# Causal masks of the third and fourth chunk pair as products on TensorE, with the first part of the hand-written order rearranged

## The chip, the cores and the metric

The kernel runs on one core of one Trainium2 chip. The metric is the device time of one execution in microseconds (us); lower is better. A core has five engines that work beside each other and wait for one another by semaphores: TensorE (PE, matrix products; the loads of its stationary operand are shown as PEld), VectorE (DVE), ScalarE (ACT), GpSimd (POOL) and SyncE (SP), whose queue here issues nearly all DMAs.

## The reference

Two layers in a row: a gated state-space scan in chunks (batch 4, 8 heads, 768 tokens, head size 32, state size 16), and a feed-forward block (3072 tokens, model size 256, hidden size 1536). The three weight matrices come as float64.

```python
for c in range(nc):                                   # chunks of 32 tokens
    cum = np.cumsum(la, axis=-1)                      # la = log(clip(a))
    L = np.exp(cum[:, :, :, None] - cum[:, :, None, :])
    L = L * causal                                    # causal: i >= j
    M = np.einsum('bhin,bhjn->bhij', Cc, Bc) * L
    y_intra = np.einsum('bhij,bhjd->bhid', M, xc)
    y_inter = np.einsum('bhin,bhnd->bhid', Cc, state) * decay_to_i[:, :, :, None]
    y[:, :, sl] = y_intra + y_inter
    state = decay_full[:, :, None, None] * state + np.sum(Bx, axis=2)
...
x = y.transpose(0, 2, 1, 3).reshape(3072, 256)
xn = x / np.sqrt(np.mean(x * x, axis=-1, keepdims=True) + 1e-06) * rms_g
g = xn @ w_gate
out = (g * (1.0 / (1.0 + np.exp(-g))) * (xn @ w_val)) @ w_out
```

## The kernel before, in words

**Work.** The scan is computed in chunks of 128 tokens, and for later pairs in halves of 64; two chunks are a *pair*, and there are twelve pairs. Two pairs make a token block of 512 tokens, and the feed-forward block runs on the six of them in turn. The steps of block 0, which also hold the scan of pairs 2 and 3, are the start of everything: constants are built, the weights are fetched in 18 pieces and made from float64 into float32 by hand, and the scan's first pairs run meanwhile.

**Order.** Nothing is scheduled by a planner. One long string, `order`, names the steps, as `block:kind.numbers/slot`, and a loop at the end of the kernel calls each in turn. Each step issues its instructions on its engines' queues, so that string is the order of work on every engine and on SP's DMA queue; an engine that waits holds up all that is queued behind it. Tiles come from pools with a fixed number of buffers, and a new tile waits until the buffer that it is given is free. The number behind the slash is one of three slots, each a pair of PSUM banks, that a step takes and a later one gives back.

**Steps that matter here.**
- `fetch.k` issues the DMA of weight piece k into one of six buffers (`wr`). Pieces 0 and 1 hold 128 columns of both the gate and the value matrix; pieces 2 to 11 hold 256 columns of one of them in turn (2 gate, 3 value, 4 gate and so on); 12 to 17 are the output matrix. `man.k` (DVE, lines 216 and 219) takes the mantissa, `pow.k` (ACT, three passes, line 197) the power of two, and `wt.k` (DVE, line 225) multiplies the two into the float32 weight.
- `bc.p` and `x.p` fetch B, C and x of pair p; `scale.p` (DVE, line 514) scales B; `turn.p` transposes B and C on PE, and `T`, `Tt`, `Td` bring them to SBUF. `rowout`, `rowe`, `dT` and `spread` send rows of decays to DRAM and back in another shape.
- `r.k` and `parts.k` make sums of logs and split them in two bfloat16 parts on DVE (lines 384 to 391). `sums` (lines 461 and 468) adds them up in PSUM for each head by small products, and `exp` (line 476) takes the exponential into the tile `L`.
- **The mask.** For pairs 0 and 1 `mask` first writes, for each chunk, the product of an identity with `whole16`, which is 0 where i >= j and -2^100 elsewhere, so that the exponential is 0 there (line 447). For pairs 2 and 3 there is no such product: `sums` opens the banks itself, and after the exponential `causal` (line 482) selects on GpSimd, once for each half of 64 partitions, over 16 x 64 elements a partition. Pairs from 4 on get their decays another way and use the same `causal`.
- `g` and `gg` are the products of B and C, and `L` and `L1` multiply them by the decays on DVE (lines 612 to 624). `A` and `S` carry the state, `y` is the output of a pair, `sq`, `yt`, `ms`, `rs`, `xn` the norm (`rs` takes the roots on ACT, line 809; `xn.0` is line 831 on DVE).
- `early.f.s` are the first gate and value products of columns f on half s of the tokens, made before the norm is known (line 855); `norm.f` corrects them (line 866). `gate.f` (line 845) does columns 2 to 5 after the norm. From column 6 on, block 0, like all later blocks, uses a product scheme with seven products for eight: `P.k.j` (line 931), `take` (line 937), `C` (line 943), `silug` and `hidg`, with weight sums by `cw` on DVE or `cwp` on GpSimd (line 900) and token sums by `tx` or `txp` (line 908). `o.f` is the output product (line 963).

Of the kernel before, what the change touches and what calls it, by code (L numbers as in the profile page):

```python
# [20 lines left out]
def kernel(  # L21
# [423 lines left out]
    def mask(e):  # L445
        for i in range(2):
            nc.tensor.matmul(out=e[:, i], lhsT=ident16,
                             rhs=whole16.unsqueeze(1).to_broadcast([P, 4, P]),
                             start=True, stop=False, skip_group_check=True)

    def sums(p, half, e):
# [6 lines left out]
        for k, h in enumerate(heads):  # L458
            for i, r in enumerate(rows_of):
                for u in parts:  # L460
                    nc.tensor.matmul(out=e[u, i, k * n:(k + 1) * n],
                                     lhsT=sel[r, h:h + 1].to_broadcast([32, n]),
                                     rhs=row[r, 0, u], start=p >= 2 and k == 0, stop=False,
                                     tile_position=(r.start, u.start), skip_group_check=True)
# [759 lines left out]
    def of_chunk(n, fn):  # L1224
# [31 lines left out]
        0:idle.7 0:x.0 0:hmask 1:exps 0:head 0:fetch.0 0:never 0:whole16 0:mask.0.0/0 0:aT  # L1256
        0:mask.1.1/2 0:gcol 0:part 0:fetch.2 0:after 0:part2 0:tmask 0:sel 0:upto 0:mean 0:mid
        0:mask.0.1/1 0:mids 0:la0 0:log4.4.2 0:log4.0.4 0:r.0 0:log 0:after2 0:x.1 0:upto2 0:parts.0
        0:d 0:dx 0:eps 0:scale.0 0:middles 0:c*2 0:turn.0 0:fetch.1 0:sums.0.1 0:cx 0:Tb.0 0:exp.0.1
        0:sums.0.0 0:exp.0.0 0:turn.1 0:Tt.1.0 0:Tt.1.1 0:T.0 0:T.1 0:last.0 0:g.0.1/1 0:Tl.0  # L1260
        0:scale.1 0:pow.0 0:cc 0:man.0 0:bc.2 0:L.0.1 0:g.0.0/0 0:fetch.5 0:A.0 0:sums.1.1 0:exp.1.1
        0:S.0 0:last.1 0:row.1 0:L.0.0 0:mask.1.0/1 0:sums.1.0 0:man.2 0:rowout.1 0:wt.0 0:exp.1.0
        0:rowe.1 0:g.1.1/0 0:Tl.1 0:g.1.0/2 0:log4.6.2 0:L.1.0 0:A.1 0:y.0/1 0:fetch.3 0:L.1.1 0:S.1
        0:y.1/2 0:pow.2 0:sq.0 0:yt.0 0:sq.1 0:man.1 0:row.0 0:rowe.0 0:r.1 0:parts.1 0:early.0.0/0
        0:bc.3 0:yt.1 0:ms.0 0:wt.2 0:scale.2 0:sums.3/1 0:pow.1 0:sums.2/2 0:pow.5 0:exp.3
        0:rowout.0 0:rs.0 0:tok 0:fetch.8 0:tokout 0:man.3 0:pow.3 0:early.0.1 0:wt.1 0:early.1.0/1
        0:dT.3 0:xn.0 0:turn.2 0:norm.0 0:T.2 0:turn.3 0:T.3 0:Tt.3.1 0:fetch.4 0:dT.2 0:man.5
        0:early.1.1 0:fetch.9 0:exp.2 0:Tt.2.0 0:fetch.7 0:wt.3 0:wt.5 0:Tt.2.1 0:norm.1 0:tx.0.0
        0:Tt.3.0 0:Td.3 0:Td.2 0:man.4 0:fetch.6 0:gate.2/0 0:silu.0 0:hid.0 0:gg.2/1 0:L1.2.3
        0:L1.2.2 0:L.2.0 0:pow.4 0:wt.4 0:man.7 0:gate.3/2 0:pow.7 0:wt.7 0:ydone.1 0:fetch.11  # L1270
        0:cwp.1.0 0:man.9 0:man.8 0:gate.4/1 0:silu.2 0:hid.2 0:x.2 0:pow.8 0:wt.8 0:txp.0.1 0:pow.9
        0:man.6 0:A.2 0:silu.3 0:x.3 0:wt.9 0:pow.6 0:hid.3 0:gate.5/0 0:S.2 0:cwp.4.0 0:silu.4
        0:scale.3 0:table.1 0:y.2/2 0:hid.4 0:silu.5 0:wt.6 0:cwp.3.0 0:hid.5 0:ydone.0 0:tx.0.2
        0:pow.11 0:S.3 0:cw.3.1 0:man.11 0:sq.2 0:bc.4 0:switch.1 0:P.2.3 0:switch.0 0:P.1.3 1:dT.0
        0:take.1.3 0:C.11.3 0:P.1.4 0:take.1.4 0:P.2.4 0:C.11.4 0:yt.2 0:x.4 0:silu.1 0:P.6.3
        0:take.6.3 0:cwp.3.2 0:tx.0.3 0:cw.4.1 0:fetch.10 0:gg.3/2 1:table 0:wt.11 0:P.5.3 0:P.7.3
        0:cwp.3.3 0:man.10 0:pow.10 0:wt.10 0:bc.5 0:cwp.5.0 0:take.7.3 0:C.22.3 0:fetch.14
        0:silug.22.3 0:silug.11.4 0:L1.3.3 0:P.5.4 0:L1.3.2 0:P.6.4 0:take.6.4 0:scale.5 0:L.3.0
        0:P.4.3 0:silug.21.3 0:P.3.3 0:scale.4 0:hidgp.11.4 0:cwp.4.2 0:fetch.12 0:pow.12
        0:hidg.21.3 0:cw.4.3 0:x.5 0:C.12.3 0:silug.12.3 0:y.3/2 0:silug.11.3 0:P.7.4 0:take.7.4  # L1280
        0:cw.5.1 1:dT.1 0:cwp.5.2 1:S.0 0:fetch.15 0:P.1.5 0:P.2.5 0:hidg.12.3 0:cwp.5.3 1:spread.0
        0:P.4.4 0:fetch.13 0:spread.10 0:take.1.5 0:P.6.5 0:table.0 0:spread.11 1:S.1 0:C.11.5
        0:C.22.4 0:sq.3 0:yt.3 0:ms.1 0:rs.1 0:cwp.1.2 0:man.12 0:take.6.5 0:P.5.5 0:wt.12 0:cwp.1.1
        0:hid.1 0:P.3.4 0:man.13 0:hidgp.11.3 1:turn.1 0:silug.21.4 0:P.7.5 0:take.7.5 1:spread.1
        0:o.0/2 0:cw.0.0 0:hidg.22.3 0:man.15 0:o.1 0:P.4.5 0:C.22.5 0:hidg.21.4 0:pow.13 0:wt.13
        0:P.3.5 0:C.12.4 0:silug.22.4 0:hidgp.22.4 0:man.14 0:silug.21.5 0:silug.22.5 0:silug.11.5
        0:C.12.5 0:pow.14 0:hidg.21.5 0:fetch.17 0:pow.15 0:o.2 0:cw.0.1 0:rb.1 0:o.3 0:xn.1 1:P.1.0
        0:silug.12.5 0:wt.14 0:hidgp.11.5 0:man.17 1:bc.0 1:take.1.0 1:P.1.1 0:tx.1.0 1:P.2.1 1:T.1
        0:txp.1.1 0:o.4 0:tx.1.2 1:take.1.1 1:P.6.1 0:pow.17 1:cw.2.0 0:hidgp.22.5 0:tx.1.3 1:C.11.1
        1:silu.11.1 1:P.6.0 1:sub.0 1:P.2.0 0:wt.15 0:wt.17 1:turn.0 1:C.11.0 0:cwp.0.2 1:Tt.1.0  # L1290
        1:hid.11.1 1:take.6.0 1:P.7.0 1:take.7.0 1:take.6.1 1:silu.11.0 1:P.5.1 1:P.5.0 1:P.4.0
        1:C.22.0 0:cwp.0.3 0:fetch.16 1:silu.21.0 0:spread.9 1:P.7.1 1:P.3.0 1:cwp.2.2 1:hid.21.0
        0:ydone.3 0:silug.12.4 1:take.7.1 1:hid.11.0 1:cwp.2.1 0:o.5 1:P.1.3 1:Tt.1.1 1:Td.1
        0:cw.1.3 1:C.22.1 1:P.4.1 1:bc.1 1:P.3.1 0:man.16 0:hidg.12.5 0:o.6 0:o.7 1:T.0 1:Tt.0.0
        0:subp.9 1:twop.2 0:hidg.12.4 0:pow.16 0:subp.11 1:take.1.3 1:C.12.0 1:silu.12.0 1:silu.21.1
        1:hidp.12.0 1:silu.22.0 1:hid.21.1 0:wt.16 1:two.0 1:two.1 1:x.0 1:silu.22.1 1:two.4
        1:C.12.1 1:twop.6 1:hid.22.0 0:ex.9 1:P.2.3 1:P.1.2 1:C.11.3 1:P.6.3 1:ex.0 1:silu.11.3
        1:P.2.2 1:take.1.2 1:P.5.3 1:hid.11.3 1:silu.12.1 1:scale2.1 1:take.6.3 1:P.7.3 1:take.7.3
        1:C.22.3 1:hid.12.1 0:o.8 1:P.6.2 0:sub.10 1:twop.3 1:take.6.2 1:C.11.2 1:two.9 1:P.4.3
        1:silu.21.3 1:two.8 1:cwp.2.3 1:hid.21.3 0:o.9 1:P.1.4 1:silu.11.2 1:hid.11.2 1:spread.3  # L1300
        1:sub.3 1:ex.3 1:P.3.3 1:take.1.4 1:twop.5 1:Tt.0.1 1:Td.0 1:C.12.3 1:silu.12.3 1:hidp.12.3
        0:ex.10 2:dT.0 1:P.5.2 1:P.6.4 1:take.6.4 1:P.7.2 1:take.7.2 0:ex.11 1:P.2.4 0:o.10 0:o.11
        1:C.22.2 1:silu.22.2 1:spread.2 1:P.4.2 1:two.10 1:silu.22.3 0:spread.8 0:subp.8 0:put.0
        1:P.3.2 0:put.1 0:put.2 1:hidp.22.1 0:ydone.2 1:C.11.4 1:silu.11.4 1:P.5.4 1:P.7.4 1:sub.2
        1:silu.21.2 1:hid.21.2 1:hid.11.4 1:hidp.22.3 0:put.3 0:ex.8 0:exps 1:hidp.22.2 1:scale2.0
        2:dT.1 1:P.1.5 1:g 1:C.12.2 1:ex.2 1:L1.3 1:take.1.5 1:P.6.5 1:take.7.4 1:C.22.4 1:twop.7
        1:silu.22.4 1:P.2.5 1:P.4.4 1:take.6.5 1:L 1:L1.2 1:P.7.5 1:y.0 1:C.11.5 1:silu.21.4
        1:hid.21.4 1:x.1 1:silu.11.5 1:P.5.5 1:two.11 1:take.7.5 1:hid.22.4 1:O.2.0 1:hid.11.5
        1:silu.12.2 1:hidp.12.2 1:u.0 1:P.4.5 1:silu.21.5 1:O.2.1 1:O.15.0 1:O.15.1 1:w.0 1:w.2
        1:C.22.5 1:silu.22.5 2:S.0 1:y.1 1:hid.21.5 1:u.1 1:O.3.0 1:u.2 2:bc.1 1:u.3 1:O.3.1 2:S.1  # L1310
        1:O.0.0 1:O.0.1 2:spread.2 2:spread.1 1:subp.1 1:P.3.5 1:C.12.5 1:sq 1:up.4 1:w.4 1:O.17.0
        1:O.17.1 1:yt 1:silu.12.5 1:hid.12.5 1:w.5 1:up.5 1:ms 1:rs 1:hidp.22.5 1:P.3.4 1:C.12.4
# [146 lines left out]
```

## Time and profile before

| what | value |
|---|---|
| time, median of 3 runs | 396.28 us (396.26 to 396.57) |
| the profiled execution's own time | 397.5 us |
| its span, first to last instruction | 395.8 us |
| PE busy, share of the span | 387.3 us, 98% |
| DVE busy | 287.4 us, 73% |
| ACT busy | 233.6 us, 59% |
| POOL busy | 155.5 us, 39% |
| granted TensorE clock | 1.000 |

The span leaves out what lies before the first and behind the last instruction, 1.7 us in the profiled execution. Busy shares are averages over the whole span; the views by stage, further down, part the start (constants, weights, first pairs) from the rest. A row of the timeline reads: start, duration, engine, line, operation, output <- inputs, shapes, count, and in brackets the idle time of the engine before it with what ended it. Rows of one line that follow each other are merged, so "x8" is eight instructions from the first one's start to the last one's end.

### The profile page before, as it was taken

How to read it: one execution, taken by the hardware profiler on the slowest of the kernel's cores; microseconds unless marked ns; L12 is line 12 of the kernel's file. 1: busy time of each engine (PE TensorE's matmuls, PEld its weight loads, DVE VectorE, ACT ScalarE, POOL GpSimd, SP SyncE). 2: the span in 40 equal slices, each digit the busy share in tenths (PEclk: the TensorE clock that was granted, in tenths of full speed). 3: DMA queues.
4: the chain of work that ended last, by engine and by line, in shares of the span. 5: the costliest groups of instructions: out<-in, count | busy, mean ns of one | idle time of the engine just before them, and what ended most of it. 6: DMA issues, size and time to landing. Idle time of an engine off the chain costs nothing.

```text
span 395.8 us, 9624 instructions
## 1 busy us (share of the span) xinstructions
PE 387.3 (98%) x3833; PEld 333.0 (84%) x3833; DVE 287.4 (73%) x594; ACT 233.6 (59%) x483; POOL 155.5 (39%) x172
## 2 busy tenths in 40 slices
...
GB/s 101 189 165 295 181 216 190 132 154 71 23 1 68 57 87 131 84 2 30 107 36 82 13 2 68 2 15 36 42 1 3 0 8 27 55 0 2 2 2 53
DMA packets 92533, 27.01 MB, mean 68 GB/s; under 512 B 77416, under 2 KB 86344, under 8 KB 92488
## 3 DMA queue, kind: packets, MB, share of 16 engines
...
q10 hardware_dynamic: 2080, 0.13, 0.4%
...
## 4 chain that ended last, share of the span: by engine, by line
PE 80%; DVE 7%; ACT 6%; issue 2%; SPq 2%; DMA 2%; POOL 0%; DVEq 0%; ACTq 0%
PE gate L931 28%; PE o L1052 20%; PE val L931 20%; PE o L963 5%; PE y L716 3%; ACT e L197 3%; DMA wr<-in_moe_w_val_dram 2%; PE g L579 1%; SPq L125 1%; DVE wgv L225 1%; DVE m L219 1%; PE tp L529 1%; ACT u L197 1%; DVE L L618 1%; DVE ob L1083 1%
## 5 line engine op out<-in xcount | busy, mean ns | idle before, releaser
L943 DVE TENSOR_TENSOR c<-val,p 128x512 f32<-128x512 f32 x99 | 67.3, 686 | 40.4 <-PE val L931 28.6
L937 ACT COPY p<-gate 128x512 f32<-128x512 f32 x99 | 56.7, 583 | 57.1 <-PE gate L931 55.6
L956 POOL TENSOR_TENSOR hid<-c 128x256 f32<-128x256 f32 x40 | 33.6, 847 | 90.4 <-ACT c L197 88.2
L931 PE MATMUL gate<-tx,wgv 128*128 128x256 f32 x264 | 65.9, 382 | 0.0
L197 ACT ACTIVATE c<-c 128x256 f32<-128x256 f32 x99 | 39.1, 415 | 30.5 <-DVE c L943 30.1
L931 PEld LDWEIGHTS gate<-tx,wgv 128*128 128x128 f32 x264 | 48.9, 190 | 7.2 <-issue 0.3
L956 DVE TENSOR_TENSOR hid<-c 128x256 f32<-128x256 f32 x59 | 28.5, 492 | 16.9 <-ACT c L197 16.9
L1083 DVE TENSOR_TENSOR ob<-ob,o 128x128 f32<-128x128 f32 (+1 forms) x90 | 24.4, 298 | 21.1 <-PE o L1052 17.7
L482 POOL TENSOR_SCALAR_AFFINE_SELECT L<-L 64x512 f32<-64x512 f32 (+1 forms) x36 | 28.2, 783 | 21.7 <-ACT L L197 19.0
L1052 PE MATMUL o<-two,hid 128*128 128x128 f32 x280 | 36.3, 276 | 0.3 <-DVE ob L1083 0.2
L1052 PEld LDWEIGHTS o<-two,hid 128*128 128x128 f32 x280 | 34.4, 192 | 1.5 <-DVE ob L1083 0.4
L931 PE MATMUL val<-tx,sw 128*128 128x256 f32 x132 | 34.0, 382 | 0.0
L931 PE MATMUL val<-xn,sw 128*128 128x256 f32 x132 | 33.7, 380 | 0.0
L931 PE MATMUL val<-xn,wgv 128*128 128x256 f32 x132 | 33.3, 380 | 0.2 <-ACT u L197 0.2
L931 PE MATMUL gate<-tx,sw 128*128 128x256 f32 x132 | 33.4, 381 | 0.0
L931 PE MATMUL gate<-xn,wgv 128*128 128x256 f32 x132 | 32.9, 379 | 0.0
L197 ACT ACTIVATE u<-gate 128x256 f32<-128x256 f32 (+1 forms) x37 | 14.8, 403 | 22.8 <-PE gate L931 20.9
L931 PEld LDWEIGHTS val<-tx,sw 128*128 128x128 f32 x132 | 24.8, 190 | 4.0 <-DVE c L943 0.5
L931 PEld LDWEIGHTS val<-xn,wgv 128*128 128x128 f32 x132 | 24.9, 190 | 3.6 <-ACT u L197 0.3
L931 PEld LDWEIGHTS gate<-tx,sw 128*128 128x128 f32 x132 | 24.6, 190 | 3.4 <-issue 0.2
L931 PEld LDWEIGHTS gate<-xn,wgv 128*128 128x128 f32 x132 | 24.6, 190 | 3.2
L931 PEld LDWEIGHTS val<-xn,sw 128*128 128x128 f32 x132 | 24.5, 190 | 3.2 <-issue 0.2
(196 smaller groups left out, 738.5 us busy)
## 6 DMA issues: line engine op xcount, KB each, us to landing
...
wr<-in_moe_w_out_dram SPq DMA_DIRECT2D x6, 512.0 KB
...
wr<-in_moe_w_gate_dram SPq DMA_DIRECT2D x5, 512.0 KB, 8.0
wr<-in_moe_w_val_dram SPq DMA_DIRECT2D x5, 512.0 KB, 4.6
...
```

The lines of the kernel that those rows point to most:

```text
L125: queue.dma_start(out=st[p][name][:, i], in_=src[b, :, sl, :].rearrange("h s n -> s h n"))
L197: nc.scalar.activation(**operands)
L219: nc.vector.scalar_tensor_tensor(out=f, in0=lo.bitcast(U32), scalar=2.0 ** -32, in1=m, op0=ALU.mult, op1=ALU.add)
L482: nc.gpsimd.affine_select(out=L[r], in_=L[r], pattern=[[0, L.shape[1]], [1, HC]], compare_op=ALU.is_ge, fill=0.0, base=0, channel_multipli ...
L716: nc.tensor.matmul(out=y[2 * k + u][rows, (2 * n + i) * HC:(2 * n + i + 1) * HC], start=(k, u, rows.start) not in opened, stop=True, skip_ ...
L931: nc.tensor.matmul(out=dst[:, half[w]], lhsT=lhsT, rhs=rhs, start=(k in (1, 2, 5) and w == 0), stop=True, skip_group_check=True)
L937: nc.scalar.copy(out=t, in_=Xs[j])
L943: nc.vector.tensor_tensor(out=t, in0=Zs[j], in1=a, op=ALU.add)
L956: engine.tensor_tensor(out=hid[:, 2 * j + c // 10 - 1, c % 10 - 1], in0=u, in1=src[:, half[1]], op=ALU.mult)
L963: nc.tensor.matmul(out=o, lhsT=hid[:, f, k // 2, (k % 2) * P:(k % 2 + 1) * P], rhs=wo[:, f], start=opens, stop=(f == NF - 1), skip_group_c ...
L1052: nc.tensor.matmul(out=Os[blk, b][:, place * P:(place + 1) * P], lhsT=hidden_or_sum(u)[:, g], rhs=rhs, start=(blk, b) not in opened, stop= ...
L1083: nc.vector.tensor_tensor(out=o, in0=o, in1=src, op=ALU.add if what[0] == "+" else ALU.subtract)
```

## The change

The masks of pairs 2 and 3 become products like those of pairs 0 and 1: a new constant `never16` (128 x 64, bfloat16) holds the mask of a 64-token half in each half of the partitions, two copies on DVE make it (`mask16`), and `mask.2` and `mask.3` write two products each (128 x 512, bfloat16) into the slot that `sums` then adds to. The two selections on GpSimd behind each of `exp.2` and `exp.3` are gone (four instructions). `sums` no longer takes a slot nor opens the banks.

The order's steps from the 14th to about the 310th are rearranged: 311 steps become 314 (`never16`, `mask.2` and `mask.3` are new). Among them some change their engine: from DVE to GpSimd go the token sums `tx.0.0` and `tx.0.3`, the weight sums `cw.4.1`, `cw.4.3`, `cw.5.1` and the products `hidg.12.3` and `hidg.22.3`; from GpSimd to DVE go the weight sums `cwp.4.0`, `cwp.3.2`, `cwp.1.1`, `cwp.1.2` and the product `hidgp.11.4`. The steps from `0:o.1 0:P.4.5` on are the same as before.

```diff
+    never16 = const.tile([P, HC], BF16, name="never16")
...
+    def mask16():
+        for r in halves:
+            nc.vector.tensor_copy(out=never16[r], in_=never[r, r])
...
-    def mask(e):
+    def mask(p, e):
+        m = [P, 4, P] if p < 2 else [P, NH, HC]
         for i in range(2):
             nc.tensor.matmul(out=e[:, i], lhsT=ident16,
-                             rhs=whole16.unsqueeze(1).to_broadcast([P, 4, P]),
+                             rhs=(whole16 if p < 2 else never16).unsqueeze(1).to_broadcast(m),
                              start=True, stop=False, skip_group_check=True)
...
-                                     rhs=row[r, 0, u], start=p >= 2 and k == 0, stop=False,
+                                     rhs=row[r, 0, u], start=False, stop=False,
...
         activation(out=L.rearrange("p i h m -> p i (h m)"), in_=e, func=AF.Exp)
-        if p >= 2:
-            causal(L.rearrange("p i h m -> p (i h) m"))
...
-    def start_decays(p, half):
+    def start_decays(p, half=0):
         ps["e", p, half] = e = take("e", ("e", p, half))
-        mask(e)
-
-    def sums_of_decays(p, half=0):
-        if p >= 2:
-            ps["e", p, half] = take("e", ("e", p, half))
-        sums(p, half, ps["e", p, half])
+        mask(p, e)
...
-        "sums": sums_of_decays,
+        "sums": lambda p, half=0: sums(p, half, ps["e", p, half]),
```

The first part of the new order (the steps up to `gate.2`; before it the 13 unchanged ones from `0:warm` to `0:idle.7`):

```
0:gcol 0:x.0 0:never 0:after 0:fetch.0 0:fetch.1 0:x.1 0:whole16 0:mask.0.0/0
0:part 0:hmask 0:upto 0:mid 0:mids 0:part2 0:aT 0:mask.1.1/2 0:la0 0:log4.0.4 0:upto2 0:r.0
0:fetch.2 0:head 0:sel 0:middles 0:after2 0:fetch.3 0:log4.4.2 0:log4.6.2 0:bc.3 0:tmask
0:parts.0 0:log 0:c*2 0:cx 0:mask.0.1/1 0:turn.0 0:Tb.0 0:T.0 0:d 0:dx 0:sums.0.1 0:sums.0.0
0:exp.0.1 0:never16 1:exps 0:exp.0.0 0:turn.1 0:scale.1 0:last.1 0:cc 0:scale.0 0:T.1 0:mean
0:g.0.1/1 0:Tt.1.0 0:g.0.0/0 0:Tt.1.1 0:L.0.1 0:L.0.0 0:sums.1.1 0:exp.1.1 0:row.1
0:rowout.1 0:man.0 0:bc.2 0:mask.1.0/1 0:sums.1.0 0:rowe.1 0:g.1.1/0 0:L.1.1 0:Tl.1
0:g.1.0/2 0:exp.1.0 0:L.1.0 0:fetch.4 0:last.0 0:Tl.0 0:fetch.7 0:dT.2 0:tok 0:tokout 0:A.1
0:A.0 0:S.0 0:S.1 0:pow.0 0:wt.0 0:y.0/1 0:sq.0 0:pow.1 0:y.1/2 0:sq.1 0:row.0 0:yt.0
0:man.1 0:wt.1 0:mask.3/1 0:rowe.0 0:yt.1 0:ydone.1 0:r.1 0:man.3 0:scale.3 0:eps
0:early.0.0/0 0:early.0.1 0:rowout.0 0:ms.0 0:parts.1 0:pow.3 0:pow.2 0:wt.3 0:rs.0
0:mask.2/2 0:scale.2 0:man.2 0:wt.2 0:sums.3 0:sums.2 0:exp.3 0:turn.2 0:T.2 0:Tt.2.0 0:xn.0
0:turn.3 0:norm.0 0:T.3 0:Tt.3.1 0:Tt.2.1 0:fetch.5 0:Tt.3.0 0:exp.2 0:Td.2 0:early.1.0/1
0:early.1.1 0:dT.3 0:man.4 0:table.1 0:x.2 0:norm.1 0:man.5 0:Td.3 0:silu.0 0:hid.0 0:pow.4
0:gate.2/0
```

The same stretch before:

```
0:x.0 0:hmask 1:exps 0:head 0:fetch.0 0:never 0:whole16 0:mask.0.0/0 0:aT
0:mask.1.1/2 0:gcol 0:part 0:fetch.2 0:after 0:part2 0:tmask 0:sel 0:upto 0:mean 0:mid
0:mask.0.1/1 0:mids 0:la0 0:log4.4.2 0:log4.0.4 0:r.0 0:log 0:after2 0:x.1 0:upto2 0:parts.0
0:d 0:dx 0:eps 0:scale.0 0:middles 0:c*2 0:turn.0 0:fetch.1 0:sums.0.1 0:cx 0:Tb.0 0:exp.0.1
0:sums.0.0 0:exp.0.0 0:turn.1 0:Tt.1.0 0:Tt.1.1 0:T.0 0:T.1 0:last.0 0:g.0.1/1 0:Tl.0
0:scale.1 0:pow.0 0:cc 0:man.0 0:bc.2 0:L.0.1 0:g.0.0/0 0:fetch.5 0:A.0 0:sums.1.1 0:exp.1.1
0:S.0 0:last.1 0:row.1 0:L.0.0 0:mask.1.0/1 0:sums.1.0 0:man.2 0:rowout.1 0:wt.0 0:exp.1.0
0:rowe.1 0:g.1.1/0 0:Tl.1 0:g.1.0/2 0:log4.6.2 0:L.1.0 0:A.1 0:y.0/1 0:fetch.3 0:L.1.1 0:S.1
0:y.1/2 0:pow.2 0:sq.0 0:yt.0 0:sq.1 0:man.1 0:row.0 0:rowe.0 0:r.1 0:parts.1 0:early.0.0/0
0:bc.3 0:yt.1 0:ms.0 0:wt.2 0:scale.2 0:sums.3/1 0:pow.1 0:sums.2/2 0:pow.5 0:exp.3
0:rowout.0 0:rs.0 0:tok 0:fetch.8 0:tokout 0:man.3 0:pow.3 0:early.0.1 0:wt.1 0:early.1.0/1
0:dT.3 0:xn.0 0:turn.2 0:norm.0 0:T.2 0:turn.3 0:T.3 0:Tt.3.1 0:fetch.4 0:dT.2 0:man.5
0:early.1.1 0:fetch.9 0:exp.2 0:Tt.2.0 0:fetch.7 0:wt.3 0:wt.5 0:Tt.2.1 0:norm.1 0:tx.0.0
0:Tt.3.0 0:Td.3 0:Td.2 0:man.4 0:fetch.6 0:gate.2/0
```

106 lines of the change are left out of this document (47 added, 59 removed).

## The prediction

> **What bounds the kernel now.** I read the page's first two lines, then busy time by stage, cut where the work changes (columns: length, busy PE, PEld, DVE, ACT, POOL with counts, granted clock, DMA share, GB/s).
>
> ```profile
> span 395.8 us, 9624 instructions
> ...
> PE 387.3 (98%) x3833; PEld 333.0 (84%) x3833; DVE 287.4 (73%) x594; ACT 233.6 (59%) x483; POOL 155.5 (39%) x172
> ```
> ```profile
> 10.00:22.00 12.00, 11.20 (x201) 7.49 (x196) 11.54 (x24) 10.70 (x19) 1.54 (x2) 1.00 0.82 167
> 22.00:34.30 12.30, 11.14 (x121) 8.84 (x121) 11.72 (x21) 11.15 (x19) 3.91 (x3) 1.00 0.84 208
> 34.30:52.40 18.10, 17.89 (x218) 8.46 (x216) 17.60 (x36) 16.03 (x26) 5.11 (x6) 1.00 1.02 235
> ...
> 76.00:396.00 320.00, 315.46 (x2977) 283.23 (x2975) 217.25 (x434) 171.15 (x371) 129.90 (x133) 1.00 0.19 42
> ```
>
> From 76 us on PE is the bound: 315 of 320 us, weight loads 283, DVE 217. From 10 to 34.3 it is not: weight loads fill 16.3 of 24.3 us, and it is DVE (23.3 of 24.3) with ACT (21.9) that works without a break. GpSimd has 5.5 us of work there. After 34.3 PE has no holes left to speak of, though DVE is as full. So a change in this prefix is worth what it moves the moment at which PE enters its unbroken stretch; three places on PE's row mark it.
>
> ```profile
> 25.27 0.44 PE L461 MATMUL e<-row,sel 32*64 32x64 bf16 x32
> 25.55 0.39 PE L468 MATMUL e<-sel,row 32*64 32x512 bf16 x4
> ...
> 29.91 1.97 PE L855 MATMUL gate<-yt,wgv 128*128 128x256 f32 x8 [0.84 <-DVE wgv L225]
> ...
> 32.59 1.89 PE L855 MATMUL gate<-yt,wgv 128*128 128x256 f32 x8
> 34.32 3.60 PE L845 MATMUL gate<-xn,wgv 128*128 128x512 f32 x8
> ...
> 52.40 1.10 PE L931 MATMUL val<-xn,wgv 128*128 128x256 f32 x4 [0.16 <-ACT u L197]
> ```
> ```profile
> 76.75 1.03 PE L931 MATMUL gate<-tx,wgv 128*128 128x256 f32 x4
> ```
>
> `gate.2` begins at 34.32, `P.2.3` at 52.40, `P.4.5`, from which on both orders are the same, at 76.75. The last real hole is the 0.84 us before 29.91: `early.1.0` waits for the weight that DVE makes in `wt.1` (line 225). Why that was late stands in the rows of DVE and POOL.
>
> ```profile
> 12.09 0.43 DVE L216 TENSOR_SCALAR m<-wr 128x512 int32<-128x512 int32 x1 [0.25 <-DMA wr<-in_moe_w_val_dram]
> ...
> 13.17 1.22 DVE L618 TENSOR_TENSOR L<-g,L 128x1024 f32<-128x1024 f32 x1
> ```
> ```profile
> 25.48 0.68 DVE L225 SCALAR_TENSOR_TENSOR wgv<-m,e 128x512 f32<-128x512 f32 x1
> 26.08 0.42 DVE L514 TENSOR_TENSOR Bd<-br,d_sb 128x256 f32<-128x256 f32 x1
> ...
> 27.07 0.43 DVE L216 TENSOR_SCALAR m<-wr 128x512 int32<-128x512 int32 x1 [0.37 <-DMA wr<-in_moe_w_val_dram]
> 27.54 0.69 DVE L219 SCALAR_TENSOR_TENSOR m<-wr,m 128x512 f32<-128x512 uint32 x1
> 28.14 1.62 DVE L225 SCALAR_TENSOR_TENSOR wgv<-m,e 128x512 f32<-128x512 f32 x1
> 29.69 2.15 DVE L831 TENSOR_TENSOR xn<-yt,sq 128x1024 f32<-128x1024 f32 x1
> ...
> 34.02 2.22 DVE L225 SCALAR_TENSOR_TENSOR wgv<-m,e 128x512 f32<-128x512 f32 x2
> ...
> 55.56 1.10 DVE L219 SCALAR_TENSOR_TENSOR m<-wr,m 128x512 f32<-128x512 uint32 x1
> ```
> ```profile
> 27.95 2.83 POOL L482 TENSOR_SCALAR_AFFINE_SELECT L<-L 64x1024 f32<-64x1024 f32 x2 [4.28 <-ACT L L197]
> 34.52 2.72 POOL L482 TENSOR_SCALAR_AFFINE_SELECT L<-L 64x1024 f32<-64x1024 f32 x2 [3.75 <-ACT L L197]
> ...
> 40.66 0.73 POOL L908 TENSOR_TENSOR tx<-xn,tx 128x256 f32<-128x256 f32 x1
> ...
> 55.19 0.93 POOL L768 TENSOR_TENSOR sq<-sq 128x256 f32<-128x256 f32 x1 [2.12 <-ACT sq L197]
> ```
>
> The same operation on line 225 takes 0.68 at 25.48 and 1.62 at 28.14, inside the selections' 27.95 to 30.78; `xn.0` takes 2.15, where a pass of 1024 elements (13.17) takes 1.22; two `wt` inside the second pair of selections take 2.22 for about 1.29 (0.68 and 0.61, the step from 25.48 to 26.08). GpSimd's selections cost DVE 0.94 + 0.93 + 0.93 = 2.8 us, in the one stretch where DVE is the bound.
>
> **The change, part by part.** *Selections out.* DVE gets 1.87 us back before `gate.2` and 0.93 behind it. On GpSimd itself 5.55 us go that held nobody else up.
>
> The Trainium skill, "SBUF — State Buffer", section "Who interferes with whom", gives the mechanism: a DVE operation with two inputs in SBUF and a GpSimd operation that reads SBUF exclude each other, the one that comes second waiting in full. By that rule the work newly put on GpSimd would cost DVE in its turn; that is weighed as a rival below.
>
> *Masks in.* Four products of 512 columns.
>
> ```profile
> 3.59 0.17 DVE L361 MEMSET mean<- 128x128 f32 x1
> ...
> 4.10 1.91 PE L447 MATMUL e<-whole,ident 128*128 128x512 bf16 x4
> 5.81 1.01 PE L377 MATMUL r_ps<-mids,la 128*128 128x256 f32 x2
> ...
> 11.22 1.99 PE L572 MATMUL g<-T 32*128 32x256 f32 x16
> ...
> 15.25 0.59 PE L447 MATMUL e<-whole,ident 128*128 128x512 bf16 x2
> ```
>
> The pair at 15.25 takes 0.59 to the end of its last, of which 0.38 is the length of one, so 0.21 apart: 0.43 a pair, 0.86 in all (the early ones are twice as slow, four from 4.10 to 5.81). `mask.3` waits for `yt.0` (slot 1 is `y.0`'s until then) and holds up `early.0.0`, which waits for `yt.0` too; `early.0.1` then waits for `yt.1`. `mask.2` stands before `sums.3`, which waits for `parts.1`. I cost them at nothing; without that cover it is 0.86. `never16` is two DVE copies of 64 x 64: nothing like it is in the trace; between nothing and 0.43 each, the time of the smallest pass of 128 partitions above (27.07). I take 0.3 for both, each being an eighth of that size.
>
> *The order, on DVE.* Before, `man.0` and the wait for its piece stand ahead of `L.0.1` at 13.17: without them (13.17 − 12.09 + 0.25 = 1.33) it could begin at 11.84. `never16` and `mean` (0.17) now stand there, 0.5. Against that, `mask.0.1` no longer precedes `r.0` on PE (two of the four in 1.71 us, 0.85), of which the logs ahead of `r.0` leave about 0.4. So `L.0.1` at about 12.0, and not below 11.84 − 0.4.
>
> From there to the end of `xn.0` DVE took 31.84 − 13.17 = 18.67. In the new order the same stretch also holds `man.0` (1.08), `wt.3` (0.61) and `scale.3` (0.34: 26.08's 0.42 less the 0.08 by which neighbouring rows overlap), and drops the selections' 1.87 and the 0.37 of waiting for piece 3, which is now fetched ahead of `bc.3`: 18.67 + 2.03 − 2.24 = 18.46. `xn.0` ends at 30.5 in place of 31.84, with `wt.3` and `scale.3` done as well. Behind `parts.1` lie `wt.3`, `scale.2`, `man.2`, `wt.2`, `xn.0`: 0.61 + 0.34 + 1.07 + 0.61 + 1.22 = 3.85, so `parts.1` ends at 26.6.
>
> *The order, on ACT and PE.*
>
> ```profile
> 24.72 0.74 ACT L197 ACTIVATE e<-wr,kinks 128x512 int16<-128x512 int16 x1
> ...
> 26.87 1.00 ACT L197 ACTIVATE L<-e 128x1024 f32<-128x1024 f32 x1
> 27.77 0.68 ACT L197 ACTIVATE sq<-ms,eps 128x512 f32<-128x512 f32 x1
> ...
> 35.56 1.28 ACT L189 ACT_TABLE_LOAD   x1
> ```
>
> A `pow` takes 26.87 − 24.72 = 2.15, an `exp` 0.9, `rs.0` two passes like 27.77's, 1.3. `early.1.0` now takes the slot that `exp.3` empties, and ACT gets there late: `L.0.0` frees slot 0 at 12.0 + 2.3, `g.1.1` and `g.1.0` take 2.0, and `last.0`, `Tl.0`, `tokout`, short passes for which no row stands here, an estimated 1, so ACT begins `pow.0` at 17.3. Then `pow.0`, `.1`, `.3`, `.2` (8.6), two squares and `rowe.0` (none longer than 27.77's, an estimated 1.3) and `rs.0` (1.3): 28.5, later than `sums.3` (26.6 + 0.2 + 0.67 = 27.5), so `exp.3` ends at 29.4. `early.1.0` and `early.1.1` follow without a break (1.73 each, as 32.59 to 34.32), `turn.2` and `turn.3` lie before them: `gate.2` at 29.5 + 3.5 = 33.0, 1.3 earlier. Its inputs are there (`xn.0` 30.5, both weights before).
>
> From `gate.2` to `P.2.3` PE has the same products, 18.08 us; DVE comes into it with what it gained plus the 0.93 of the second selections, and ACT with `pow.5` more to do (2.15) but its table load and what follows about as much earlier. I keep 18.1 there, and let 0.2 of the remaining holes go by `P.4.5`. On SP's queue the fetches of pieces 1, 3, 4 and 7 and `bc.3` are moved ahead, pieces 5, 8, 9, 6, 11 and `x.2`, `x.3` behind `dT.2` and the row stores. Sum: −1.5 us. The profiled execution of 397.5 becomes 396.0; it lies 1.22 above the median of 396.28, so **394.8** for the median.
>
> **Rivals.** A measurement of this kernel can tell about 0.2%, 0.8 us, from no change: below 395.5 counts as faster, above 397.1 as slower.
>
> *The block comes back under other work.* Seven steps go from DVE to GpSimd and five the other way, two more of 0.73 (40.66) there. For: at 55.56 line 219 took 1.10, not 0.69, beside the 0.93 of POOL at 55.19. Against: DVE's inputs often come from PSUM, and it saves two passes of 0.4. Two full blocks eat 1.46 of 1.5: 396.2. That is what the section of the Trainium skill named above would give, and 55.56 agrees with it.
>
> *A fetch comes too late (slower).* There are six buffers for pieces. If they are given as they fall free, piece 6 gets piece 4's, which is free when ACT has done `pow.4`: behind `exp.3` (29.4) lie six short copies of the transposes (an estimated 0.4 each), `exp.2` (0.9), the table load (1.28), `silu.0` (under 0.7) and `pow.4` (2.15): 36.8.
>
> ```profile
> 32.96 1.45 SPq L167 DMA_DIRECT2D wr<-in_moe_w_gate_dram  x1
> ```
> ```profile
> wr<-in_moe_w_gate_dram SPq DMA_DIRECT2D x5, 512.0 KB, 8.0
> wr<-in_moe_w_val_dram SPq DMA_DIRECT2D x5, 512.0 KB, 4.6
> ```
>
> Before, it was issued at 32.96. Queued behind it on SP are `x.3`, pieces 11, 10, 12 and `bc.5`. DVE comes to `man.6` after ten passes of 0.61, four `man` of 1.07 and five short ones of 0.34, 12.1 behind `xn.0`'s 30.5: 42.6. With the 4.6 us from issue to landing of one row the piece is there at 41.4 and nothing is lost; with the 8.0 of the other at 44.8, DVE, full until then, loses 2.2, and PE gets the weight for `P.2.3` as much later: 397.0, and 397.6 if the pieces behind it add a quarter of that again. It eats the gain from a landing of 6.5 us on and makes the kernel slower from 8.1 on. Against: SP's held queue leaves the DMAs empty, so the short one is nearer.
>
> *PE is the bound all along.* By the 98% of the page's first part the masks' 0.86 come on top and nothing else counts: 397.1. Against: 29.91's wait, and weight loads at two thirds. The Trainium skill, "Perfetto Trace Analysis", section "Identifying the Most-Contended Engine", holds matmul busy time a bad measure and the loads' a good one; by it, too, PE has room there.
>
> **How the numbers follow.** Forecast (gain of 0.8 to 3): 0.60. Block back, or lead lost to a fetch just too late, 395.5 to 397.1: 0.18. Late fetch and slower: 0.13; PE bound, just over the limit: 0.09. Lower end: 1.5 + 0.93 (second selections) + 0.7 (of PE's holes of 0.84 and 0.16 all but the 0.3 that is counted) is 3.1, so 393.2. Upper end 397.4, inside the late fetch. Beyond these lie under 2 in 10.
>
> **What would show it.** Right: no select near 28 and 35, line 225 at 0.68 and `xn.0` near 1.2 there; `L.0.1` by 12.2, `gate.2` by 33.3, `P.2.3` by 51.2, `P.4.5` by 75.3; the mask rows without a wait behind them. Wrong: `gate.2` not before 34, a DVE wait for a weight piece near 43, or PE waits between 33 and 75 over 1 us in sum.

## The result, and the profile after

| | before | after |
|---|---|---|
| median of 8 runs | 396.42 us (395.85 to 397.56) | 395.37 us (394.90 to 396.09) |
| the profiled execution | 397.5 us, span 395.8 | 395.41 us, span 393.7 |

The ratio is 0.9967, with a 95% interval of 0.9955 to 0.9978: about 1.3 us faster, 1.05 by the medians. The traces differ by 2.1 us, since the profiled execution of before lies 1.1 above its median and that of after on it.

First the page's head and the busy time by stage, as shown for before (length, busy PE, PEld, DVE, ACT, POOL with counts, clock, DMA share, GB/s).

```profile
span 393.7 us, 9631 instructions
...
PE 386.9 (98%) x3837; PEld 332.2 (84%) x3837; DVE 285.3 (72%) x594; ACT 234.1 (59%) x483; POOL 151.8 (39%) x170
```
```profile
10.00:22.00 12.00, 11.35 (x197) 8.07 (x197) 11.37 (x23) 10.68 (x19) 1.10 (x1) 1.00 0.94 221
22.00:34.30 12.30, 12.23 (x122) 9.02 (x121) 11.93 (x24) 12.11 (x21) 3.32 (x4) 1.00 0.82 197
34.30:52.40 18.10, 18.09 (x224) 9.34 (x223) 17.65 (x38) 16.78 (x27) 1.12 (x1) 1.00 1.01 258
```

The page's shares hardly move. In the stages PE is now full from 22 us on (12.23 of 12.30, before 11.14), and POOL keeps 3.32 us of work there though the selections are gone. PE's timeline has the marks that the prediction named:

```profile
21.03 0.59 PE L453 MATMUL e<-never,ident 128*128 128x512 bf16 x2
...
21.89 3.62 PE L859 MATMUL gate<-yt,wgv 128*128 128x256 f32 x16
...
26.22 0.59 PE L453 MATMUL e<-never,ident 128*128 128x512 bf16 x2
...
28.90 3.70 PE L859 MATMUL gate<-yt,wgv 128*128 128x256 f32 x16
32.45 3.60 PE L849 MATMUL gate<-xn,wgv 128*128 128x512 f32 x8
35.97 1.13 PE L583 MATMUL g<-T 32*64 32x128 f32 x32
...
49.85 1.13 PE L935 MATMUL val<-xn,wgv 128*128 128x256 f32 x4
```
```profile
74.42 0.38 PE L935 MATMUL gate<-tx,wgv 128*128 128x256 f32 x1
```

`gate.2` starts 1.87 us earlier (34.32 before), `P.2.3` 2.55, `P.4.5` 2.33; the hole of 0.84 before `early.1.0` is gone. DVE, POOL and ACT:

```profile
9.01 0.38 DVE L313 CAST never<-never 64x64 bf16<-64x64 f32 x2
...
11.90 2.36 DVE L622 TENSOR_TENSOR L<-g,L 128x1024 f32<-128x1024 f32 x2 [0.33 <-PE g L576]
...
26.35 0.48 DVE L396 SCALAR_TENSOR_TENSOR row<-second,third_part,rest 128x256 bf16<-128x256 bf16 x1
...
28.94 0.69 DVE L225 SCALAR_TENSOR_TENSOR wgv<-m,e 128x512 f32<-128x512 f32 x1
29.55 1.22 DVE L835 TENSOR_TENSOR xn<-yt,sq 128x1024 f32<-128x1024 f32 x1
...
32.70 1.10 DVE L219 SCALAR_TENSOR_TENSOR m<-wr,m 128x512 f32<-128x512 uint32 x1
...
35.97 0.42 DVE L557 TENSOR_TENSOR T<-tp,dT 128x256 f32<-128x256 f32 x1
```
```profile
30.85 0.73 POOL L912 TENSOR_TENSOR tx<-xn 128x256 f32<-128x256 f32 x1 [7.51 <-DVE xn L835]
31.66 1.59 POOL L912 TENSOR_TENSOR tx<-xn,tx 128x256 f32<-128x256 f32 x2
```
```profile
16.42 0.79 ACT L197 ACTIVATE e<-wr,kinks 128x512 int16<-128x512 int16 x1
...
27.82 1.02 ACT L197 ACTIVATE L<-e 128x1024 f32<-128x1024 f32 x1
```

Line 225 takes 0.69 where it took 1.62, `xn.0` 1.22 where it took 2.15. In their place line 219 takes 1.10 beside the token sums on POOL (0.69 elsewhere).

Cut at four marks, the profiled executions of all kernels stand as follows (us): the start of `L.0.1`, then the stretches from there to `gate.2`, on to `P.2.3` and on to the end of the span. The runs came in four sets, each on one chip with runs of the kernel before beside it; the ratio is that of each set and not the quotient of the two medians. The expected times below were written with a kernel before at 396.4 us in mind; where it has 397.6 or 397.4, the ratio is what can be compared.

| kernel | `L.0.1` | to `gate.2` | to `P.2.3` | to the end | median (runs) | before in its set | ratio, 95% |
|---|---|---|---|---|---|---|---|
| before | 13.17 | 21.15 | 18.08 | 343.39 | 396.42 (8) | | |
| after | 11.90 | 20.55 | 17.40 | 343.83 | 395.37 (8) | 396.42 | 0.9967, 0.9955 to 0.9978 |
| masks, old order | 12.93 | 20.56 | 17.92 | 343.84 | 396.70 (12) | 396.38 | 1.0002, 0.9987 to 1.0017 |
| selections, new order | 11.51 | 22.01 | 18.56 | 343.71 | 397.53 (9) | 396.38 | 1.0032, 1.0019 to 1.0044 |
| after + useless selections | 11.51 | 21.99 | 18.56 | 343.85 | 397.97 (6) | 396.38 | 1.0041, 1.0026 to 1.0056 |
| after + memsets on POOL | 11.52 | 20.55 | 17.97 | 343.82 | 396.19 (12) | 396.38 | 0.9995, 0.9982 to 1.0008 |
| after again | 12.01 | 20.54 | 17.51 | 343.70 | 395.84 (10) | 397.58 | 0.9951, 0.9932 to 0.9970 |
| masks twice | 11.88 | 21.17 | 16.87 | 343.81 | 395.47 (7) | 397.58 | 0.9938, 0.9915 to 0.9961 |
| new order to `gate.2` | 12.44 | 20.54 | 18.70 | 342.94 | 396.27 (12) | 397.58 | 0.9956, 0.9940 to 0.9973 |
| old order to `gate.2` | 13.18 | 20.88 | 18.68 | 343.81 | 397.76 (12) | 397.58 | 1.0009, 0.9991 to 1.0028 |
| before again | 13.15 | 21.08 | 19.04 | 343.42 | 397.66 (12) | 397.42 | 1.0005, 0.9982 to 1.0029 |
| no masks at all | 11.60 | 20.53 | 17.63 | 343.66 | 395.64 (12) | 397.42 | 0.9952, 0.9935 to 0.9970 |
| `Td.3` first | 11.96 | 20.54 | 17.96 | 343.79 | 396.35 (12) | 397.42 | 0.9973, 0.9956 to 0.9990 |
| `Td.3` first, `gg.3` later | 11.51 | 20.54 | 20.29 | 343.82 | 396.78 (12) | 397.42 | 0.9978, 0.9956 to 0.9999 |

Between the two first traces: 1.27 us are won up to `L.0.1`, 0.60 to `gate.2`, 0.68 to `P.2.3`, and 0.44 are lost behind it.

### The profile page after: what moved, and what is told of

Same layout as the page of the kernel before. It is cut to its first block, busy times and chain, and to the rows that moved or that the text cites. A ratio compares the mean times of both kernels' runs of the same rounds, so it can differ in the third digit from the quotient of the medians.

```text
span 393.7 us, 9631 instructions
## 1 busy us (share of the span) xinstructions
PE 386.9 (98%) x3837; PEld 332.2 (84%) x3837; DVE 285.3 (72%) x594; ACT 234.1 (59%) x483; POOL 151.8 (39%) x170
## 4 chain that ended last, share of the span: by engine, by line
PE 81%; DVE 11%; issue 4%; ACT 3%; DVEq 0%; ACTq 0%
PE gate L935 27%; PE o L1056 21%; PE val L935 20%; PE o L967 4%; PE y L720 3%; PE g L583 1%; DVE wgv L225 1%; DVE m L219 1%; DVE m L216 1%; PE tp L533 1%; DVE hid L882 1%; PE g L576 1%; PE e L453 1%; PE y L648 1%; DVE S L672 1%
## 5 line engine op out<-in xcount | busy, mean ns | idle before, releaser
L486 POOL TENSOR_SCALAR_AFFINE_SELECT L<-L 64x512 f32<-64x512 f32 x32 | 23.0, 718 | 13.5 <-ACT L L197 10.9
```

The source lines that it names most:

```text
L486: nc.gpsimd.affine_select(out=L[r], in_=L[r], pattern=[[0, L.shape[1]], [1, HC]], compare_op=ALU.is_ge, fill=0.0, base=0, channel_multipli ...
```

## The experiments

Two theories stood at first: the gain comes from DVE, which the selections no longer hold up (A); or it comes from the new order alone, with the masks beside the point (B).

**Masks in the old order.** The change's code, with the order of before and only the three new steps put in.

```diff
+0:never16
 0:scale.0
...
+0:mask.3/1
 0:ms.0
...
-0:sums.3/1
+0:mask.2/2 0:sums.3
...
-0:sums.2/2
+0:sums.2
```

> The masks as products in the order of before: never16 stands ahead of scale.0, mask.3 ahead of ms.0, mask.2 ahead of sums.3, all else as before. Theory A (the selections held DVE up, and that was half of the gain): line 225 at 28 us back to 0.68, xn.0 to 1.2, gate.2 between 33.4 and 33.9 in place of 34.32, the time 0.4 to 0.9 us below before. Theory B (the order alone brings the gain, the masks are an exchange of one cost for another): the four products of 0.43 a pair show on PE ahead of sums.3, and the time is between before and 0.9 above it.

Measured 396.70 us, 1.0002: no gain. The trace shows the block gone: two rows of DVE.

```profile
28.92 1.22 DVE L835 TENSOR_TENSOR xn<-yt,sq 128x1024 f32<-128x1024 f32 x1 [0.81 <-ACT sq L197]
...
37.03 0.42 DVE L557 TENSOR_TENSOR T<-tp,dT 128x256 f32<-128x256 f32 x1 [1.39 <-DMA dT<-rowe]
```

`xn.0` takes 1.22, but waits 0.81 for ACT's roots: in the old order DVE reaches it before its input. In this trace `gate.2` comes 0.83 us earlier than in before's, 0.59 of it in the stretch from `L.0.1`. Behind it DVE waits 1.39 us for a transfer from DRAM (the second row), and the stretch to `P.2.3` is only 0.16 shorter; from there to the end 0.45 are lost again. A second trace of the same steps (the old order to `gate.2`, further down) has the first of these stretches 0.27 shorter, not 0.59. So in the old order the selections' end alone is worth 0.3 to 0.6 us up to `gate.2`, where the prediction counted 1.87 us of DVE time, and by the medians nothing: the interval leaves room for 0.5 us, and 0.4 to 0.9 were expected.

**Selections in the new order.** The code of before with the new order, without the three mask steps.

```diff
-0:never16
-0:mask.3/1
-0:mask.2/2
-0:sums.3
+0:sums.3/1
-0:sums.2
+0:sums.2/2
```

> The selections on GpSimd back, in the order of after (without never16 and the two mask steps; sums takes the slots as before). Theory A: the selections now lie at 28.8 to 31.6 and 31.8 to 34.5, wt.2 and xn.0 are blocked, xn.0 ends about 1.8 later (32.6), gate.2 at 32.8 to 33.5, and the time is 0.5 to 1.2 us above after. Theory B: the time is that of after or up to 0.5 below it, for PE has four products less.

Measured 397.53 us, 1.0032 (1.0019 to 1.0044): slower than before, against theory B. Beside the changed kernel's 0.9967, from another set, that is about 2.6 us more, where theory A had expected 0.5 to 1.2. POOL, DVE and PE of this kernel:

```profile
28.51 2.68 POOL L482 TENSOR_SCALAR_AFFINE_SELECT L<-L 64x1024 f32<-64x1024 f32 x2 [5.57 <-PE tp L529]
31.43 3.05 POOL L482 TENSOR_SCALAR_AFFINE_SELECT L<-L 64x1024 f32<-64x1024 f32 x2 [0.23 <-ACT L L197]
```
```profile
28.56 1.63 DVE L225 SCALAR_TENSOR_TENSOR wgv<-m,e 128x512 f32<-128x512 f32 x1
30.11 2.15 DVE L831 TENSOR_TENSOR xn<-yt,sq 128x1024 f32<-128x1024 f32 x1
...
33.72 1.04 DVE L216 TENSOR_SCALAR m<-wr 128x512 int32<-128x512 int32 x1
34.79 1.09 DVE L219 SCALAR_TENSOR_TENSOR m<-wr,m 128x512 f32<-128x512 uint32 x1
```
```profile
33.52 3.70 PE L845 MATMUL gate<-xn,wgv 128*128 128x512 f32 x8 [1.31 <-DVE hid L866]
...
38.69 0.65 PE L579 MATMUL g<-T 32*64 32x128 f32 x20 [0.99 <-DVE T L553]
```

The second selections end at 34.48; the 1.09 of line 219 at 34.79 is beside the token sums that follow them on POOL, and the changed kernel has the same (1.10). In the new order the blocked passes end as holes in PE's work: 1.31 us before `gate.2`, 0.99 in the products of `gg.2`.

**Useless selections beside the masks.** The changed kernel, with the four selections issued as before, but written into a part of `hid` that is filled only later.

```diff
+        if p >= 2:
+            spare(L.rearrange("p i h m -> p (i h) m"))
...
+    def spare(L):
+        scratch = hid[:, 10:12].rearrange("p f k (a m) -> p (f k a) m", m=HC)
+        for r in halves:
+            nc.gpsimd.affine_select(out=scratch[r], in_=L[r], ...)
```

> After, with four selections of the old shape at the old places on GpSimd, which read L and write a part of hid that is filled only later; nothing waits for them but the next writer of L. They do no useful work. Theory A: DVE is blocked as in the run with the selections back, 0.5 to 1.2 us above after. If the old cost was the wait of line 612 and the like for the selections' results and not the block, the time is within 0.2 us of after.

Measured 397.97 us, 1.0041 (1.0026 to 1.0056); its marks are those of the kernel above within 0.2 us. So it isn't that `L` was ready late: the selections cost by running.

**Writes in their place.** The same, with one copied element of each partition (so that they start at the same time) and three memsets of 128 x 1024 in place of each pair of selections.

```diff
+        nc.gpsimd.tensor_copy(out=scratch[:, 0, 0:1], in_=L[:, 0, 0:1])
+        for k in range(3):
+            nc.gpsimd.memset(scratch, float(k))
```

> After, with GpSimd kept busy at the same places by writes alone (a one-element copy of L, then three memsets of 128x1024 into a part of hid that is filled later, no useful work), about as long as the selections or longer. If only a GpSimd operation that reads SBUF blocks DVE's two-input operations: within 0.3 us of after, wt.2 near 0.68 and xn.0 near 1.2. If any work on GpSimd does: 0.5 to 1.2 us above after, as with the selections beside.

Measured 396.19 us, 0.9995 (0.9982 to 1.0008): 1.78 us below the kernel with the selections, on the same chip, but no gain over the kernel before that stands clear of noise, where the changed kernel's time within 0.3 us had been expected. POOL and DVE of this kernel:

```profile
28.77 2.97 POOL L490 MEMSET hid<- 128x1024 f32 x3
...
32.04 3.37 POOL L490 MEMSET hid<- 128x1024 f32 x3
```
```profile
28.57 0.69 DVE L225 SCALAR_TENSOR_TENSOR wgv<-m,e 128x512 f32<-128x512 f32 x1
29.18 1.22 DVE L843 TENSOR_TENSOR xn<-yt,sq 128x1024 f32<-128x1024 f32 x1
...
35.50 1.16 DVE L890 TENSOR_TENSOR hid<-u,hid 128x512 f32<-128x512 f32 x1
```

POOL is busy longer than with selections, and DVE beside it runs at full pace; it is held up only from 35.50 on, beside the token sums that the memsets had pushed back. The span is 393.9 against 395.9 with selections: those cost 2.05 us in this order, 1.44 by `gate.2` (33.50 against 32.07) and the rest by `P.2.3`. To `gate.2` this kernel takes what the changed one takes (20.55); on to `P.2.3` it takes 17.97 for 17.40, so the memsets are not free there. The profiled execution is 0.2 us above the changed kernel's and 0.6 below its own median; what else holds up the median no trace shows. The Trainium skill, "SBUF — State Buffer", section "Who interferes with whom", says that a DVE operation with two inputs in SBUF contends with a GpSimd operation that reads SBUF and not with one that only writes it; both halves of that show here. Theory A holds for the selections' block, but only with the new order, in which DVE is what `gate.2` and `gg.2` wait for.

**The changed kernel again.**

> The changed kernel once more, so that the others of this set stand beside it on one chip. 395.2 to 395.7 us, 0.9965 to 0.9985 of the kernel before; profiled span 393.5 to 394.0, gate.2 at 32.4 to 32.5, P.2.3 at 49.8 to 49.9, P.4.5 at 74.4 to 74.5. If the trace's marks repeat within 0.1 us, the 2.1 us by which the two traces differed, against 1.1 between the medians, come from the kernel before, whose profiled execution would then be one of its longer ones.

395.84 us, 0.9951 (0.9932 to 0.9970): the time is 0.14 us above what was expected, the ratio below it, since the kernel before is 1.2 us longer on this chip. The stretches repeat within 0.13 us.

**Masks twice.** Each mask product of pairs 2 and 3 issued twice.

```diff
-        for i in range(2):
+        for i in [0, 1] if p < 2 else [0, 1, 0, 1]:
```

> The changed kernel with every mask product of the third and fourth pair issued twice (the output stays the same): two more products of 0.22 us apart for each pair, 0.86 us in all. If the masks lie where TensorE waits anyway, as the prediction had it, the time is that of the changed kernel within 0.2 us. If TensorE is without a hole there, each adds its own length except for the hole of 0.24 us ahead of sums.3: gate.2 0.4 to 0.65 us later (32.85 to 33.1) and the time 0.4 to 0.7 us above the changed kernel's, so that the masks themselves cost about as much and the selections' end is worth that much more.

395.47 us, 0.9938; not slower than the changed kernel. PE:

```profile
21.01 1.03 PE L453 MATMUL e<-never,ident 128*128 128x512 bf16 x4
...
33.05 3.60 PE L849 MATMUL gate<-xn,wgv 128*128 128x512 f32 x8
36.58 0.69 PE L583 MATMUL g<-T 32*64 32x128 f32 x32
```

Of the 0.86 us, 0.62 arrive between `L.0.1` and `gate.2`. `gg.2` takes 0.69 us instead of 1.13, and by `P.2.3` all but 0.1 is gone (37.95 to 38.04 us from `L.0.1`). In the changed kernel `gg.2` stands for DVE's `Td.3` (35.97 to 36.39): by the code, the transposes that `Td.3` reads lie in one of the two single banks, and `gg.2` writes its last part into that one. So `gate.2` came as in the second case of the expectation (TensorE without a hole pays for each product) and the time as in the first: small stalls inside a group of products don't show as holes, and the added work went into them.

**No masks.** The changed kernel without the four products; the entries above the diagonal of pairs 2 and 3 stay in.

```diff
-        for i in range(2):
+        for i in range(2 if p < 2 else 0):
             nc.tensor.matmul(out=e[:, i], lhsT=ident16,
...
-                                     rhs=row[r, 0, u], start=False, stop=False,
+                                     rhs=row[r, 0, u], start=p >= 2 and k == 0, stop=False,
```

> The changed kernel without the four mask products (the sums then write their bank themselves, as before the change; the entries above the diagonal of the third and fourth pair stay in, so the output differs). If the masks cost nothing because DVE's chain to the products of gg.2 ends later than TensorE's own work, gate.2 starts up to 0.5 us earlier (32.0 to 32.45), P.2.3 not (L.0.1 to P.2.3 37.9 to 38.1, as in the changed kernel 37.95 and 38.05), and the time is the changed kernel's within 0.2 us. If each mask adds its 0.43 us to TensorE's work, L.0.1 to P.2.3 is 37.1 to 37.5 and the time 0.5 to 0.9 us below.

395.64 us, 0.9952, the changed kernel's ratio (0.9951) in another set. From `L.0.1` to `gate.2` it takes 20.53 us with no mask, 20.55 with. The time of the masks turns into waits for DVE ahead of `gate.2`: the sixteen products of `early.0` with what they wait for take 3.86 us up to `ms.0` (3.46 with masks, from 21.89 to 25.35), since `early.0.1` waits for `yt.1`, and `sums.3` waits 0.51 for `parts.1` (line 396). `gg.2` waits for `Td.3` here too, as it does with masks:

```profile
21.16 3.72 PE L859 MATMUL gate<-yt,wgv 128*128 128x256 f32 x16
25.02 1.10 PE L800 MATMUL ms<-sq,mean 128*128 128x512 f32 x2
26.62 0.48 PE L467 MATMUL e<-row,sel 32*64 32x64 bf16 x33 [0.51 <-DVE row L396]
...
36.37 0.65 PE L583 MATMUL g<-T 32*64 32x128 f32 x20 [0.25 <-DVE T L557]
```

**Half of the order.** Masks, the new order up to the first product of `gate.2`, from there the remaining steps as in the old order; and the reverse.

```diff
 (new order)
 ... 0:gate.2/0
-0:txp.0.0 0:cw.0.0 0:gg.2/1 ...
+(the steps that remain, in the old order and on their old engines)
```

> Masks, the new order up to the first product of gate.2, and from there the remaining steps in the old order (with the old choice of DVE or GpSimd for them). If the gain is made in the opening and then only carried along: gate.2 at 32.4 to 32.6, P.2.3 at 49.9 to 50.3, P.4.5 at 74.4 to 74.9, 395.2 to 395.8 us. If the old order behind gate.2 gives it back, as it did in the kernel with masks in the old order: P.4.5 at 75.6 to 76.4 and 396.2 to 397.2 us, with holes in TensorE's work between 34 and 75 us that the changed kernel does not have.

> Masks, the old order up to the first product of gate.2 (as in the kernel with masks in the old order), and from there the remaining steps in the new order. gate.2 at 33.4 to 33.6. If the order behind gate.2 is what keeps the gain: P.2.3 at 50.8 to 51.1, P.4.5 at 75.3 to 75.6, about 1.0 us behind the changed kernel all along, 396.0 to 396.6 us. If the opening is what counts: as masks in the old order, P.4.5 at 76.1 to 76.4, 396.5 to 397.0 us.

With the new opening 396.27 us (0.9956): 0.4 above the changed kernel beside it. With the old opening 397.76 (1.0009): nothing is left, and 1.9 above the changed kernel. By the medians the opening carries most of the gain. How much of that is the late transfer is not parted: the trace with the old opening has, ahead of `gg.2`, the wait for `dT` that the kernel with masks in the old order has (1.39 us there).

```profile
38.19 0.42 DVE L557 TENSOR_TENSOR T<-tp,dT 128x256 f32<-128x256 f32 x1 [1.63 <-DMA dT<-rowe]
```

Behind the new opening the old steps cost 1.2 to 1.3 us up to `P.2.3`, for instance in PE's wait for `hid` before `gate.5`, and give 0.8 back later:

```profile
46.12 3.70 PE L849 MATMUL gate<-xn,wgv 128*128 128x512 f32 x8 [0.47 <-DVE hid L882]
```

**Before again.**

> The kernel before once more, for a second trace of it. If its first trace is typical, the stretches repeat within 0.2 us: L.0.1 at 13.0 to 13.2, from there 21.1 to 21.3 to gate.2, 18.0 to 18.2 to P.2.3. If that execution was one of the longer ones, L.0.1 or the later stretches are shorter here and the span is 394.5 to 395.3 us.

The stretches up to `gate.2` repeat within 0.1 us, the next one not: 19.04 against 18.08. DVE and PE:

```profile
38.89 0.42 DVE L553 TENSOR_TENSOR T<-tp,dT 128x256 f32<-128x256 f32 x1 [0.87 <-DMA dT<-rowe]
```
```profile
39.37 0.65 PE L579 MATMUL g<-T 32*64 32x128 f32 x20 [0.86 <-DVE T L553]
```

In this execution the decays `dT`, which go to DRAM and back, came late, and the wait went through DVE into PE. The fetch is issued at almost the same time in both traces (31.29 and 31.22).

**An attempt to do better: `Td.3` ahead of `man.5`,** so that `gg.2` needn't stand, and with it `gg.3` behind `P.5.3`.

```diff
-0:norm.1 0:man.5 0:Td.3
+0:norm.1 0:Td.3 0:man.5
```
```diff
-0:gg.3/2 0:take.1.4 0:silug.11.3 0:C.11.4 0:L.3.0 0:take.6.3 0:cwp.3.3 0:P.5.3
+0:take.1.4 0:silug.11.3 0:C.11.4 0:take.6.3 0:cwp.3.3 0:P.5.3 0:gg.3/2 0:L.3.0
```

> The changed kernel with one DVE step moved: Td.3 ahead of man.5 instead of behind it. In the changed kernel the products of gg.2 stood from 36.16 until Td.3 had ended on DVE (36.39), since the transposes that it reads lie in the bank they write. If DVE's chain to Td.3 is what holds TensorE there, Td.3 ends at 35.3 to 35.4, gg.2 takes 0.6 instead of 1.06 us, and P.2.3 and the end come 0.35 to 0.5 us earlier (L.0.1 to P.2.3 37.5 to 37.7): 395.0 to 395.5 us where the changed kernel has 395.4 to 395.8. If the bank is held by something else, or dT.3 (its fetch issued at 31.7) lands after 35, nothing moves or P.2.3 comes later.

> As the kernel with Td.3 moved, and the products of gg.3 (with L.3.0 behind them) issued after P.5.3 instead of before: in the changed kernel they stood 0.51 us for ScalarE's squares of the second block (until 55.08). If both holes close and nothing else takes their place: 0.8 to 1.0 us below the changed kernel, first output product 0.8 to 1.0 us earlier after L.0.1 (118.1 to 118.4 us against 119.1 to 119.2), 394.5 to 395.0 us. If DVE or ScalarE are the next bound behind 56 us, 0.3 to 0.6 of that stays out.

Neither gains: 396.35 us (0.9973) and 396.78 (0.9978), where the kernel without masks in the same set has 0.9952. In the first, `gg.2` does close, but the next group that needs DVE, `y.2`, stands instead (1.33 us against 0.74 in the changed kernel); DVE had lost 0.85 us waiting for `dT.2`:

```profile
36.03 0.69 PE L583 MATMUL g<-T 32*64 32x128 f32 x32
...
48.10 1.33 PE L720 MATMUL y<-T,S 32*64 32x64 f32 x32
```
```profile
32.87 0.42 DVE L557 TENSOR_TENSOR T<-tp,dT 128x256 f32<-128x256 f32 x1 [0.85 <-DMA dT<-rowe]
```

That wait is that of `Td.2`, up to which the order is the changed kernel's, so the edit didn't make it. The second has it too (0.81), and there `Td.3` reached its place before its data:

```profile
37.01 0.43 DVE L557 TENSOR_TENSOR T<-tp,dT 128x256 f32<-128x256 f32 x1 [1.94 <-DMA dT<-rowe]
```
```profile
37.49 0.65 PE L583 MATMUL g<-T 32*64 32x128 f32 x20 [1.45 <-DVE T L557]
38.07 8.83 PE L849 MATMUL gate<-xn,wgv 128*128 128x512 f32 x16
```

Here 1.7 us of the longer stretch are something else: the 16 products take 8.83 us, 7.13 in most others, at a granted clock of 0.57 from 38 to 42 us (4 us at 0.57 lose 1.7). `gg.3` found its input ready, but PE's next products then waited 0.59 us for DVE. `man.5`, which takes 1.06 us in the changed kernel, would have covered half of the 1.94: where the transfer is late, it is cover and not idle order. With one trace of each kernel it is not shown that this alone keeps the two from gaining.

## Why the prediction was right, and where its sum was not

- **Selections and DVE's block:** right in mechanism. Line 225 at 0.69 and `xn.0` at 1.22 stand as forecast; selections bring the block back, memsets don't. The 2.8 us of DVE time are worth 2.05 of the end in the new order (1.78 by the medians) and nothing that the medians show in the old one. Of the 1.87 counted up to `gate.2`, 1.44 came out there, and only because order and masks were changed together.
- **Masks at nothing:** right, and by the covers named: without them `early.0.1` waits about 0.4 us more for `yt.1`, and `sums.3` 0.51 for `parts.1`. That `gg.2` waits for DVE's `Td.3` as well, and hides about 0.5 of a second pair of masks, wasn't seen.
- **`never16`** 0.38, forecast 0.3. **`L.0.1`** at 12.0 forecast, 11.5 to 12.4 in the traces with the new opening, 12.9 to 13.2 with the old. `parts.1` ends at 26.83 (26.6), `xn.0` at 30.77 (30.5): DVE's sum held within 0.3.
- **ACT:** forecast too late by 0.9: `pow.0` starts at 16.42, not 17.3, since from `L.0.0`'s end (14.26) it is 2.2 us, where the prediction counted 3.0 for `g.1.1`, `g.1.0` and estimated short passes. So `exp.3` ends at 28.84 instead of 29.4, when the transposes before `early.1.0` end too, and **`gate.2`** comes at 32.45, not 33.0.
- **`gate.2` to `P.2.3`, "18.1":** mis-sized; 17.40. Three groups of short products that stand for DVE or ACT got shorter: `gg.2` 1.06 from 1.23, `A.2` 0.36 from 0.48, `y.2` with the state products behind it 1.77 from 2.15. The "0.2 more by `P.4.5`" had the wrong sign: 24.57 us after `P.2.3`, before 24.35. PE's holes weren't closed there; a new one stands before `gg.3` (0.51, for ACT's squares).
- **The sum:** −1.5 forecast from trace to trace, −2.1 measured there, −1.05 by the medians of the first set and −1.74 beside the second run of the changed kernel. **The step to the median** took before's excess of 1.22 us (its profiled execution over its median) to lie outside the stretches that change, so that after's execution would have it too. It hasn't: after's lies 0.04 above its median. That step failed, and the trace difference of 2.1 contains some of that excess. Too small a sum (0.6) and an excess that didn't carry over (1.2) partly cancel, by luck, in 394.8 against 395.37.
- **Rivals.** The block under other work did come back, in one place on the path (1.10 at 32.70, 0.41 too long, ahead of `Td.3`) and in several off it: by the chain to `gg.2` it costs up to 0.4, not 1.46. The late fetch didn't occur: its two conditions fail in these rows of SP and DVE; piece 6 went out before `pow.4`'s end and `man.6` started without a wait.

```profile
34.98 0.42 SPq L167 DMA_DIRECT2D wr<-in_moe_w_gate_dram  x1
```
```profile
43.36 0.42 DVE L216 TENSOR_SCALAR m<-wr 128x512 int32<-128x512 int32 x1
```

- PE as the bound all along: refuted for these stretches by masks twice and no masks, which leave the time as it is.

Only in part is it known why before's executions spread so widely (395.85 to 397.56 here, 396.09 to 400.71 in another set). The mean granted clock of each execution tells some of it: in the last two sets 23 of 75 executions of before have 0.996 or 0.991 and take 397.3 to 400.7 us, the others 396.1 to 398.4. A mean of 0.996 is what one dip of 4 us at 0.57 makes in 396 us. Of the changed kernel, masks twice and no masks, 1 of 29 executions in these sets has it. Without these executions the changed kernel is 1.45 us below before in the third set, with them 1.74. No run shows why the old order met the lower clock more often. A late `dT` is another cause that a trace showed, but the first trace of before has neither and was long too. Nor was it shown separately how much of the gain in the median is the shorter path, how much the shorter waits for `dT` and how much the clock.
